# 32-column TensorE tiles from batch 1, sums in one bank, batch 2's sums via DRAM on two queues, and scores a quarter into a w_out group

## The chip, the cores and the metric

One core of a Trainium2 chip runs the whole program. The metric is device time in microseconds (us); "span" is the stretch from the first to the last instruction in the profile, which is about 2 us shorter than the time. One run of the kernel before differs from the next by some 0.3 us, so differences of 1 us count here.

## The reference, cut to what matters

```python
# 8 batches, 8 heads, 1024 tokens, head size 64; 64 projected keys
k_proj, v_proj = E @ k, F @ v                       # per head: 64 x 64
attn = softmax(q @ k_proj.T / 8)                    # 1024 x 64 per head
x = (attn @ v_proj), heads side by side             # 8192 tokens x 512
h = x @ w_in                                        # 512 -> 2048
out = (h * clip(h + 3, 0, 6) / 6) @ w_out           # 2048 -> 512
```

By far the most work is in the two products with w_in and w_out: 32 and 8 groups per batch, 256 rounds of a 128x128 by 128x512 product (a round is the time in which all tiles that lie side by side do one matmul each). The attention of the next batch is woven in between.

## The kernel before

The dense products go through one helper. It cuts the stationary operand into column tiles, which run side by side in the array (the tile form in the views, such as 128*64, is rows by columns):

```python
width = [P // 2]                                    # 64 columns
def in_columns(ps, stationary, moving, **flags):
    for lo in range(0, stationary.shape[-1], width[0]):
        nc.tensor.matmul(ps[lo:lo + width[0]], stationary[:, lo:lo + width[0]], moving, **flags)
```

The softmax denominators are made in two ways. In the "visits" (batches 1 and 2) they are summed with 64x64 matmuls against ones, straight into the layout that the products need. From batch 3 on each head's sum is made once, and the reciprocals go through DRAM and come back as broadcasts:

```python
def all_sums(self, alloc):                          # 8 matmuls of 32 columns, two banks
    ...
def spread(self, den):
    few = att.tile([P, 2, TOK], f32, ...)
    inverse(few, den)                               # Ln and Exp(-x) on ScalarE
    rows = dram.tile([H, NB, TOK], f32, ...)
    nc.sync.dma_start(out=rows..., in_=few[::16])
    self.recs = [rec_tile() for _ in range(KO)]
    for h in range(H):                              # 8 x 256 KB, all from the SP queue
        nc.sync.dma_start(out=self.recs[h // 2]..., in_=rows[h:h + 1]....to_broadcast([D, NB * TOK]))
```

Loads are chained: `turn` transposes a batch's keys (kT) and queries (qT) by DMA, waits for them on GpSimd ("mark"), and only then lets the loads of the next batch start. In block b TensorE does w_in and w_out of batch b, and the attention of batch b + 1 sits at fixed places n = 0 to 7 between the groups.

The softmax here doesn't subtract the row's maximum and nothing guards it: scores larger than these inputs give would overflow.

## Time and profile before

| | kernel before |
|---|---|
| time, median of 3 | 507.14 us (507.04 to 507.15) |
| span | 505.5 us |
| TensorE busy / VectorE / ScalarE | 99% / 48% / 51% |
| instructions of the program, in 16 KB fetches | 38 |

The busy share says that TensorE never rests, and not what it does: a change of tile form or a slower round counts as busy. The lines that show where TensorE loses time stand in the prediction.

```profile
q8 instruction: 38, 0.62, 0.5%
```

### The profile page before, as it was taken

The numbers are of one execution on the slowest core, as the hardware profiler recorded it, in microseconds if no ns is written. First come the engines' busy times: TensorE is split into PE (matmuls) and PEld (weight loads), VectorE is DVE, ScalarE is ACT, GpSimd is POOL, SyncE is SP. The second block draws the span as 40 slices with busy tenths as digits, with TensorE's granted clock in tenths as the row PEclk, the third lists the DMA queues.
The fourth block names the chain that finished last, engine by engine and source line by source line (L and its number), as shares of the span: only waits on it lengthen the run. The fifth ranks groups of instructions, "written<-read, shape, count | busy, mean of one in ns | idle before, by whom it ended". The sixth has DMA issues, their size and how long they took to land.

```text
span 505.5 us, 11242 instructions
## 1 busy us (share of the span) xinstructions
PE 498.9 (99%) x4858; PEld 259.5 (51%) x4858; DVE 245.1 (48%) x384; ACT 256.1 (51%) x438; POOL 38.7 (8%) x58
## 2 busy tenths in 40 slices
PE   8999999999999999999999999999999999999997
PEld 4554554554454555545554555545555555555554
DVE  3572736865733564536635455533752446334420
ACT  3757466566565444653555544654455544344431
POOL 8620020020020020020001000000000000000000
PEclk9999999999999999999999999999999999999999
DMA  9999979799299999699416992248110361101112
GB/s 168 198 205 208 200 131 231 142 155 202 73 151 194 230 169 190 137 154 249 123 43 118 205 249 69 61 100 209 43 43 29 82 164 43 39 26 43 43 43 84
DMA packets 78074, 66.30 MB, mean 131 GB/s; under 512 B 36216, under 2 KB 67192, under 8 KB 78024
## 3 DMA queue, kind: packets, MB, share of 16 engines
q0 software_dynamic: 32480, 29.36, 37.4%
q1 hardware_dynamic: 45320, 35.89, 27.7%
q8 instruction: 38, 0.62, 0.5%
q10 hardware_dynamic: 224, 0.33, 0.2%
q14 instruction: 12, 0.10, 0.1%
HBM read 69.73 MB, written 16.94 MB: 171 GB/s over the span
## 4 chain that ended last, share of the span: by engine, by line
PE 85%; DMA 12%; POOL 2%; ACT 1%; issue 0%; DVE 0%; ACTq 0%; POOLq 0%
PE mm L172 79%; DMA q<-in_q_dram 6%; DMA w_in_sb<-in_moe_w_in_dram 2%; PE at L172 2%; DMA v<-in_v_dram 2%; DMA qT<-q 2%; PE at L251 1%; PE at L233 1%; PE mm L251 1%; POOL q L106 1%; PE mm L271 1%; POOL k L110 1%; ACT aT L242 0%; PE mm L233 0%; POOL v L110 0%
## 5 line engine op out<-in xcount | busy, mean ns | idle before, releaser
L512 DVE SCALAR_TENSOR_TENSOR g<-r,mm 128x512 bf16<-128x512 f32 x256 | 173.5, 686 | 178.7 <-ACT r L511 177.9
L172 PE MATMUL mm<-w_out_sb,g 128*64 128x512 bf16 (+2 forms) x2080 | 235.0, 376 | 0.2 <-DVE g L512 0.2
L172 PE MATMUL mm<-xT,w_in_sb 128*64 128x512 bf16 x2048 | 231.5, 379 | 0.3
L511 ACT ACTIVATE r<-mm 128x512 f32<-128x512 f32 x256 | 152.2, 599 | 74.5 <-PE mm L172 73.5
L172 PEld LDWEIGHTS <-w_in_sb 128*64 128x64 bf16 x2048 | 117.2, 110 | 104.0 <-issue 0.8
L172 PEld LDWEIGHTS <-g 128*64 128x64 bf16 x2080 | 116.2, 110 | 105.5 <-issue 7.0
L546 ACT COPY o_sb<-mm 128x512 f32<-128x512 f32 x55 | 32.2, 586 | 126.7 <-PE mm L172 126.7
L264 DVE TENSOR_TENSOR xT<-at,rec 128x512 bf16<-128x512 f32 x42 | 26.5, 681 | 6.5 <-ACT rec L184 6.5
L242 ACT ACTIVATE aT<-at 128x512 bf16<-128x512 f32 x38 | 20.2, 615 | 9.1 <-PE at L233 9.1
L208 DVE CAST kp<-at 64x512 bf16<-64x512 f32 x12 | 7.7, 677 | 15.9 <-PE at L172 15.9
L223 POOL COPY mark<-qT 1x1 bf16<-1x1 bf16 x4 | 0.7, 176 | 165.0 <-DMA qT<-q 165.0
L242 ACT ACTIVATE aT<-mm 128x512 bf16<-128x512 f32 x18 | 10.3, 613 | 3.9 <-PE mm L233 3.9
L546 DVE COPY o_sb<-mm 128x512 f32<-128x512 f32 x8 | 5.5, 687 | 13.8 <-PE mm L172 13.8
L172 PE MATMUL at<-v,f_t 128*64 128x512 bf16 x48 | 11.4, 381 | 0.3 <-DMA v<-in_v_dram 0.3
L172 PE MATMUL at<-k,e_t 128*64 128x512 bf16 x48 | 11.6, 382 | 0.0
L264 DVE TENSOR_TENSOR xT<-mm,rec 128x512 bf16<-128x512 f32 x14 | 9.0, 685 | 4.3 <-PE mm L251 4.3
L184 ACT ACTIVATE rec<-rec 128x1024 f32<-128x1024 f32 x10 | 10.6, 1060 | 0.3
L178 ACT ACTIVATE rec<-mm 128x512 f32<-128x512 f32 x10 | 5.5, 595 | 7.9 <-PE mm L251 5.4
L178 ACT ACTIVATE few<-mm 128x512 f32<-128x512 f32 x10 | 5.4, 594 | 7.4 <-PE mm L271 7.4
L93 PE MATMUL mm<-ones 128*128 128x512 bf16 x18 | 7.4, 549 | 1.5 <-DVE halves L84 1.5
L172 PEld LDWEIGHTS <-e_t 128*64 128x64 bf16 x56 | 5.7, 110 | 6.0 <-issue 1.8
L211 DVE CAST vp<-at 64x512 bf16<-64x512 f32 x12 | 8.3, 694 | 0.4
(73 smaller groups left out, 155.0 us busy)
## 6 DMA issues: line engine op xcount, KB each, us to landing
out_dram<-o_sb SPq DMA_DIRECT2D x63, 256.0 KB, 3.0
rec<-rows SPq DMA_DIRECT2D x40, 256.0 KB, 6.5
k<-in_k_dram POOLq DMA_DIRECT2D x7, 1024.0 KB, 15.0
v<-in_v_dram POOLq DMA_DIRECT2D x7, 1024.0 KB, 20.7
q<-in_q_dram POOLq DMA_DIRECT2D x7, 1024.0 KB, 10.0
w_out_sb<-in_moe_w_out_dram POOLq DMA_DIRECT2D x4, 512.0 KB, 16.0
w_in_sb<-in_moe_w_in_dram POOLq DMA_DIRECT2D x5, 256.0 KB, 9.7
k<-in_k_dram POOLq DMA_DIRECT2D x4, 256.0 KB, 5.5
```

The lines of the kernel that those rows point to most:

```text
L93: nc.tensor.matmul(ps, ones[:, :P], ones, start=True, stop=True)
L172: nc.tensor.matmul(ps[lo:lo + width[0]], stationary[:, lo:lo + width[0]], moving, **flags)
L178: nc.scalar.activation(rec[:, i], den, AF.Ln)
L184: nc.scalar.activation(flat, flat, AF.Exp, scale=-1.0)
L208: nc.vector.tensor_copy(self.kp[:, :, a, :], self.ps[:KP].rearrange("p (h d) -> p h d", d=D))
L211: nc.vector.tensor_copy(self.vp[a * KP:(a + 1) * KP], self.ps[KP:].rearrange("p (h d) -> p h d", d=D))
L242: nc.scalar.activation(self.aT[j][:, r].rearrange("p a n -> p (a n)"), tiles[r], AF.Exp, scale=scale)
L251: nc.tensor.matmul(tiles[t][c:c + D].rearrange("p (r n) -> p r n", r=2), stationary(r, 2 * j + a), self.aT[j][r:r + KP, :, a, :], start=Tr ...
L264: nc.vector.tensor_mul(self.xT[:, j, t, :], av[t], rec[:, t])
L511: nc.scalar.activation(r, h_ps, AF.Relu, bias=0.5, scale=1.0 / 6.0)
L512: nc.vector.scalar_tensor_tensor(g[:, fo, :], r, 1.0, h_ps, op0=ALU.min, op1=ALU.mult)
L546: (copy or nc.scalar.copy)(o_sb, o_ps)
```

## The change

Its intent, as far as the code tells, is to give the sums the same tile form as the dense products, so that they need no change of form, to use the cheaper sums for batch 2 too, and to place the attention pieces where ScalarE has time to follow. Cut to its core, with long calls put in words:

```diff
-    halves = consts.tile([P, NB, KP // 4], ...)
+    halves = consts.tile([P, 2, 2, NB, KP // 8], ...)   # all heads' sums in one bank
...
+    width[0] = P // 4                # from batch 1: 32 columns
     second = Attention(2)
     for b in range(1, B):
...
-        if b == 1: visits(...) for batch 2
+        if b == 1:
+            plan = {4: (4, second.all_scores), 5: (3, second.all_sums), 6: (2, second.first_values),
+                    7: (2, lambda: second.some_values((2, 3), ((pmm, pmm), (pmm, pat))))}
+        elif b + 1 < B:
+            plan = {3 + (b == 2): (2, third.projected) ..., 4 + (b == 2): (2, values 0, 1), 6: (2, values 2, 3)}
+            if b == 2:
+                plan.update({0: (2, second.projected), 1: (4, second.all_scores), 2: (4, second.all_sums)})
+            else:
+                plan.update({0: (1, scores 1, 2, 3), 1: (4, second.all_sums)})
...
             for h in range(H):
-                nc.sync.dma_start(out=self.recs[...]
+                (nc.sync, nc.gpsimd)[h % 2].dma_start(out=self.recs[...]
...
-        if fo == 7:
+        if fo == 9:
             second.projected()       # batch 1, in block 0
```

In the plan, `n: (q, act)` means: act after quarter q of the n-th w_out group. The transpose of batch 3's queries moves from the middle of block 1 to its end, batch 1's first scores come one quarter later, and the loads of batches 5 to 7 bring keys and values before queries.

## The prediction

> **What bounds the kernel now.** I read the page's busy times and granted clock first, then the chain that ended last, then TensorE's rows in order of time, because only these show what lies between two matmuls.
>
> ```profile
> PE 498.9 (99%) x4858; PEld 259.5 (51%) x4858; DVE 245.1 (48%) x384; ACT 256.1 (51%) x438; POOL 38.7 (8%) x58
> PEclk9999999999999999999999999999999999999999
> PE 85%; DMA 12%; POOL 2%; ACT 1%; issue 0%; DVE 0%; ACTq 0%; POOLq 0%
> L172 PE MATMUL mm<-w_out_sb,g 128*64 128x512 bf16 (+2 forms) x2080 | 235.0, 376 | 0.2 <-DVE g L512 0.2
> L172 PE MATMUL mm<-xT,w_in_sb 128*64 128x512 bf16 x2048 | 231.5, 379 | 0.3
> ```
>
> TensorE is busy 99% at full clock, VectorE and ScalarE about half. The chain is TensorE too; its DMA share is the start, up to the queries of batch 1 at 68.7 us. A saving must therefore come out of TensorE's own row: its pace inside dense stretches, the loss where the kind of matmul changes, or the few waits. The timeline of TensorE (start, length, line, operation, tile form, count) has the first two:
>
> ```profile
> 299.78 3.62 PE L172 MATMUL mm<-xT,w_in_sb 128*64 128x512 bf16 x32
> 303.23 1.89 PE L172 MATMUL mm<-w_out_sb,g 128*64 128x512 bf16 x16
> 305.05 0.41 PE L251 MATMUL mm<-aT,vp 64*64 64x512 bf16 x4
> 305.29 0.39 PE L251 MATMUL at<-aT,vp 64*64 64x512 bf16 x4
> 305.51 0.39 PE L233 MATMUL at<-qT,kT 64*64 64x256 bf16 x8
> 305.83 1.92 PE L172 MATMUL mm<-w_out_sb,g 128*64 128x512 bf16 x16
> 307.58 0.60 PE L172 MATMUL mm<-xT,w_in_sb 128*64 128x512 bf16 x4
> ```
>
> Pace: 32 matmuls, in 16 rounds of two 64-column tiles side by side, go from 299.78 to 303.23: 0.2157 us a round. Change of form: 8 rounds from 303.23 should end at 304.955, but the values start at 305.05, 0.10 lost. Two rounds of values take 0.46 where 0.43 is due: 0.02 for the first round after a change. Two rounds of scores (256 columns, 0.109 each) and another 0.10 lead to 305.83; the 8 rounds after that take 1.75 instead of 1.725, again 0.02. An excursion out of the dense form and back costs 0.10 + 0.02 + 0.10 + 0.02, about 0.245 us.
>
> ```profile
> 152.66 1.89 PE L172 MATMUL mm<-w_out_sb,g 128*64 128x512 bf16 x16
> 154.49 0.61 PE L271 MATMUL mm<-aT,halves 128*32 128x512 bf16 x8
> 155.03 0.63 PE L251 MATMUL at<-aT,vp 64*64 64x512 bf16 x8
> 155.59 1.92 PE L172 MATMUL mm<-w_out_sb,g 128*64 128x512 bf16 x16
> ```
>
> Here the sums (32-column tiles) and the values make two forms in one excursion, with three changes. The sums take 0.54 to the next start: two rounds (0.43), one change (0.10) and 0.01 for the first round, not 0.02. Such an excursion costs about 0.357 us. Last, the waits:
>
> ```profile
> 54.70 0.38 PE L172 MATMUL at<-k,e_t 128*64 128x512 bf16 x1
> 55.42 0.38 PE L172 MATMUL at<-v,f_t 128*64 128x512 bf16 x1 [0.34 <-DMA v<-in_v_dram]
> 68.80 0.41 PE L233 MATMUL mm<-qT,kT 64*64 64x256 bf16 x8 [0.27 <-DMA qT<-q]
> 382.26 3.97 PE L172 MATMUL mm<-xT,w_in_sb 128*64 128x512 bf16 x32
> 386.39 3.64 PE L172 MATMUL mm<-w_out_sb,g 128*64 128x512 bf16 x32 [0.16 <-DVE g L512]
> ```
>
> 0.50 us for batch 1's values at 54.7, 0.34 for its queries at 68.8, and 0.65 in the last batch's score exponentials: 16 rounds from 382.26 take 4.13 instead of 3.47. A fourth of 0.17 lies inside the scores at 139.5.
>
> **What the Trainium skill says.** "TensorEngine Tiling (Array Packing)", Key Properties: changing the tiling mode, not just the tile, drains TensorE. The trace agrees: 0.10 us per change. "TensorE: Matmul & The Clock Gate", section "Wait — 56ns, not 53.3ns?": back to back, a warm matmul costs N / 2.4 GHz plus some 2.5 ns. For 512 columns that is 215.8 ns, the measured pace; two tiles at 512 columns and four at 256 (0.109) both show it, so I take it as a cost per round, whatever the number of tiles. The same section gives a rival: with hardware decode off, the sequencer spends about 62 ns per matmul; no row here rules on it. "Trainium Kernel Development and Optimization", Key Constraints: DMAs issued from several engines run on the same 16 DMA engines, and only issue time is saved. In this trace the eight broadcasts of reciprocals take the SP queue 4.9 us to issue (340.8 to 345.8).
>
> **The change part by part.**
>
> *32-column tiles.* From batch 1 on, a dense round becomes four matmuls and four weight loads instead of two and two. The pace should stay at 0.2158, so 1800 rounds gain nothing. What changes is the form: the sums now have the form of the dense matmuls and cost no change. I counted excursions in the two programs' order of instructions, after batch 1's four visits (the same in both). Before: 15 plain and 5 with sums, 15 x 0.245 + 5 x 0.357 = 5.46 us. After: 18 plain ones, and six sums inside the dense stretches. Returning to 32 columns costs 0.01 instead of 0.02, as the sums show, so 18 x 0.231 = 4.16, plus one change from 64 to 32 columns, 0.11. Saved: 1.20 us.
>
> *Batch 2's sums.* 32 matmuls of 64x64 for sums (with the values, 8 rounds) become 8 of 32 columns plus 4 rounds of values: 2 rounds fewer, 0.43 us. Putting all sums in one bank halves the ScalarE work on them (a 0.59 and a 1.06 us instruction fewer per batch), which is off the path. The round trip through DRAM must now fit in block 1. Sums end about 115 us, the exponential about 118, rows written and visible 2 us later (338.85 to 340.82), and eight broadcasts of 256 KB in 8 to 11 us more: 129 to 131 for the last. VectorE wants the first half at 128 and the rest at 131. It just fits, because loading batch 3 (3 MB, begun at 101) is over by about 120 now that the transpose of its queries no longer runs beside it.
>
> *What it makes VectorE do at the start of batch 2.* Eight products at a pitch of 0.6 us stand behind the last hardswish, from about 128.5, so the third and fourth head pairs are ready 0.15 and 0.35 us after TensorE wants them. Before, a projection of 1.73 us lay there and hid this. Given back: 0.5 us.
>
> *Scores a quarter into a w_out group.* Twelve rounds (2.6 us) now follow the scores before w_in needs a bank. Six exponentials pitched at 0.49 us start 0.4 us after the first scores and end about when the group does. The 0.65 us of the last batch goes. The 0.17 of batch 3's scores goes too, but both new all-at-once scores use all eight banks, and the last waits about 0.17 for the copy of the output just made: 2 x 0.17 against 0.17, plus 0.17.
>
> *Batch 1.* Projecting two w_in tiles later removes the 0.50 us wait for values. But it ends 0.9 us later, so the transpose of the keys, then that of the queries on the same queue, are issued about 0.6 us later than 60.27, and the scores start near 69.4 instead of 68.8, with one more quarter (0.86) done before them. Net gain 0.28 us.
>
> Sum: -1.20 - 0.43 - 0.65 + 0.17 - 0.28 + 0.50 = -1.89 us. 507.14 - 1.89 = 505.25; I predict 505.2.
>
> **The rivals.** First, the sequencer cannot feed eight instructions per 216 ns. Proven over long stretches is only four per 216 (54 ns each); bursts such as 24 score matmuls with their loads in 0.78 us (16 ns each) could come from a filled queue. At 62 ns per matmul a round would take 248 ns, some 15% on 1800 rounds: about 565 us. Against it: the sums with four tiles and the scores ran at the array's pace. Second, four tiles hide the 2.5 ns of a round: 1800 x 2.5 = 4.5 us, so about 501. Against it: four-tile scores still pay it (0.109 and not 0.107). Third, batch 2's reciprocals come late. In this trace the time from writing the rows to the first broadcast was 2.0 to 5.9 us, the longer ones beside loads; 4 us late gives 507 to 509. Fourth, all small waits vanish, with the batch 1 gain as large as the two waits (0.84) and none at batch 2: 504.2.
>
> **Range and chances.** The removed changes and rounds (1.6 us) are nearly certain if the pace holds; the waits are worth between -1.6 and +1. So 503.6 to 506.8 holds it 8 times in 10. Faster by over 2% needs 10 us, which no part has: 0.02. Slower by over 2% needs the first rival: 0.04. Within 2%: 0.94.
>
> **What would show each step.** The dense pace in batches 4 to 6 should be 0.2158 per round of four; a cycle of one batch, 60.00 us before, should be 59.85. No gap beside the sums. TensorE near 382 without a wait, near 131 a short one on VectorE's xT. The first scores near 69.4. I am wrong if the pace per round moves by even 1 ns (1.8 us), or if TensorE waits for a broadcast.

## The result, and the profile after

| | before | after |
|---|---|---|
| time, median of 6 | 507.01 us (506.89 to 507.15) | 507.89 us (507.76 to 509.31) |
| span of the profiled run | 505.5 us | 505.8 us |
| time less span, profiled run | 1.75 us | 2.1 us |

The ratio is 1.0024 (95% interval 1.0011 to 1.0037): slower by a quarter of a per cent, where 0.4% faster was forecast. A ratio here is the mean time of one kernel's runs over that of the other's of the same rounds, so it is not quite the ratio of the medians.

The page of the changed kernel: TensorE still is the chain, but broadcasts ("rec<-rows") have entered it, and the instruction queue has nearly doubled.

```profile
PE 496.9 (98%) x8562; PEld 246.2 (49%) x8562; DVE 245.7 (49%) x384; ACT 244.3 (48%) x425; POOL 51.4 (10%) x82
q8 instruction: 67, 1.10, 0.9%
PE mm L175 85%; PE at L175 2%; DMA rec<-rows 2%; DMA w_in_sb<-in_moe_w_in_dram 2%; DMA k<-in_k_dram 1%; DMA rows<-few 1%; PE mm L254 1%; PE at L236 1%; PE mm L236 1%; PE at L254 1%; PE mm L275 1%; PE at L422 0%; POOL rec L290 0%; POOL q L109 0%; POOL k L113 0%
```

First the part of the prediction that held. TensorE's timeline in block 4 of the changed kernel (start, length, line, operation, tile form, count):

```profile
263.06 3.63 PE L175 MATMUL mm<-xT,w_in_sb 128*32 128x512 bf16 x64
266.51 3.63 PE L175 MATMUL mm<-w_out_sb,g 128*32 128x512 bf16 x64
269.96 0.61 PE L275 MATMUL mm<-aT,halves 128*32 128x512 bf16 x8
270.40 1.90 PE L175 MATMUL mm<-xT,w_in_sb 128*32 128x512 bf16 x32
```

64 matmuls, 16 rounds of four, take 3.45 us: 0.2157 a round, as with two tiles. The sums take 0.44, two rounds and nothing for a change. The starts of the single matmuls in the trace give 0.21583 in both kernels. A cycle of one batch (scores at 259.68 to scores at 319.54) is 59.86 us; 60.00 before.

The last batch's scores, a quarter into the group, no longer stop TensorE (16 rounds from 382.78 take 3.46, where the kernel before needed 4.13):

```profile
380.18 2.77 PE L175 MATMUL mm<-w_out_sb,g 128*32 128x512 bf16 x48
382.78 3.63 PE L175 MATMUL mm<-xT,w_in_sb 128*32 128x512 bf16 x64
386.24 3.63 PE L175 MATMUL mm<-w_out_sb,g 128*32 128x512 bf16 x64
```

Now what did not. TensorE at the start of block 2, where batch 2's products are needed:

```profile
128.85 1.91 PE L175 MATMUL mm<-w_out_sb,g 128*32 128x512 bf16 x32
132.63 1.48 PE L175 MATMUL mm<-xT,w_in_sb 128*32 128x512 bf16 x24 [1.87 <-DVE xT L267]
134.67 1.69 PE L175 MATMUL mm<-xT,w_in_sb 128*32 128x512 bf16 x28 [0.56 <-DVE xT L267]
```

Eight rounds from 128.85 end at 130.58, but the next start is at 132.63: 2.04 us. The six rounds from there end at 133.94, and the next start is at 134.67: 0.73. Together 2.77 us. The bracket names VectorE's products, so look there, for what VectorE waited for:

```profile
127.78 1.28 DVE L267 TENSOR_TENSOR xT<-at,rec 128x512 bf16<-128x512 f32 x2
130.16 1.29 DVE L267 TENSOR_TENSOR xT<-at,rec 128x512 bf16<-128x512 f32 x2 [1.10 <-DMA rec<-rows]
131.88 1.29 DVE L267 TENSOR_TENSOR xT<-mm,rec 128x512 bf16<-128x512 f32 x2 [0.43 <-issue]
133.93 0.69 DVE L267 TENSOR_TENSOR xT<-mm,rec 128x512 bf16<-128x512 f32 x1 [0.75 <-DMA rec<-rows]
134.53 0.68 DVE L267 TENSOR_TENSOR xT<-at,rec 128x512 bf16<-128x512 f32 x1
```

VectorE waits for broadcasts in front of the third product and of the seventh. (The 0.43 in front of the fifth ended just after another broadcast had landed, at 131.80.) And the SP queue shows why these are late:

```profile
117.52 0.53 SPq L286 DMA_DIRECT2D rows<-few  x1
122.21 2.38 SPq L290 DMA_DIRECT2D rec<-rows  x4
```

The reciprocals are written at 117.52, but the first broadcast, which waits until they are in DRAM, is issued at 122.21: 4.7 us, where I had 2.0. In the trace's DMA packets the loads of batch 3 run from 102.3 to 122.3 us, and the broadcasts' packets from 123.8 to 132.3.

### The profile page after: what moved, and what is told of

The parts are those of the page before. It is cut to its first block, busy times and chain, and to the rows that moved or that the text cites. A ratio compares the mean times of both kernels' runs of the same rounds, so it can differ in the third digit from the quotient of the medians. Undisturbed runs are those within 1.5% of the kernel's fastest.

```text
span 505.8 us, 18693 instructions
## 1 busy us (share of the span) xinstructions
PE 496.9 (98%) x8562; PEld 246.2 (49%) x8562; DVE 245.7 (49%) x384; ACT 244.3 (48%) x425; POOL 51.4 (10%) x82
## 4 chain that ended last, share of the span: by engine, by line
PE 92%; DMA 6%; POOL 1%; issue 1%; ACT 0%; DVE 0%; POOLq 0%; DVEq 0%; ACTq 0%
PE mm L175 85%; PE at L175 2%; DMA rec<-rows 2%; DMA w_in_sb<-in_moe_w_in_dram 2%; DMA k<-in_k_dram 1%; DMA rows<-few 1%; PE mm L254 1%; PE at L236 1%; PE mm L236 1%; PE at L254 1%; PE mm L275 1%; PE at L422 0%; POOL rec L290 0%; POOL q L109 0%; POOL k L113 0%
## 5 line engine op out<-in xcount | busy, mean ns | idle before, releaser
L175 PE MATMUL mm<-w_out_sb,g 128*32 128x512 bf16 (+3 forms) x3904 | 235.9, 376 | 0.0
L175 PE MATMUL mm<-xT,w_in_sb 128*32 128x512 bf16 (+1 forms) x3840 | 231.5, 379 | 2.8 <-DVE xT L267 2.4
L175 PEld LDWEIGHTS <-w_in_sb 128*32 128x32 bf16 (+1 forms) x3840 | 110.2, 98 | 113.6 <-issue 4.1
L175 PEld LDWEIGHTS <-g 128*32 128x32 bf16 (+1 forms) x3904 | 109.4, 98 | 111.5 <-issue 6.7
L290 POOL DMA_DIRECT2D rec<-rows x24 | 12.5, 531 | 194.1 <-DVE g L511 159.3
L267 DVE TENSOR_TENSOR xT<-at,rec 128x512 bf16<-128x512 f32 x31 | 19.9, 683 | 6.9 <-ACT rec L187 5.8
L267 DVE TENSOR_TENSOR xT<-mm,rec 128x512 bf16<-128x512 f32 x25 | 16.2, 687 | 6.2 <-PE mm L254 4.9
L175 PE MATMUL at<-k,e_t 128*32 128x512 bf16 (+1 forms) x104 | 13.3, 379 | 0.0
L175 PE MATMUL at<-v,f_t 128*32 128x512 bf16 (+1 forms) x104 | 13.2, 379 | 0.0
L175 PEld LDWEIGHTS <-e_t 128*32 128x32 bf16 (+1 forms) x104 | 5.8, 98 | 5.9
```

Of the source, the lines that this page charges most:

```text
L267: when(lambda t=t: nc.vector.tensor_mul(self.xT[:, j, t, :], av[t], rec[:, t]))
L290: (nc.sync, nc.gpsimd)[h % 2].dma_start(out=self.recs[h // 2][h % 2 * D:(h % 2 + 1) * D].rearrange("d t n -> d (t n)"), in_=by_head[h // 4 ...
```

## The experiments

Three theories stood against each other at first. Theory: batch 2's reciprocals come late, because the loads of batch 3 hold the DMA engines. Rival A: VectorE's eight products in a row are the wait, whenever the reciprocals come. Rival B: 32-column tiles cost something.

**1. Batch 3's loads queued earlier** (the edit in short):

```diff
-                nc.gpsimd.tensor_copy(mark, last)
-                load_kqv(self.b + 1, "qkv" if self.b == 2 else "kvq")
+                if self.b != 2: (mark; load_kqv(self.b + 1, "kvq"))
+                if self.b == 1: load_kqv(3, "qkv")
```

> The changed kernel, but the loads of batch 3 are queued right behind those of batch 2 instead of after the transpose of batch 2's keys. Theory (batch 2's reciprocals come late because the loads of batch 3 hold the DMA engines until 122.3 us, so the rows written at 117.5 are only visible at 122.1): the loads end near 112, the rows are visible about 2 us after their issue, the broadcasts end 2 to 3 us earlier, TensorE's waits at 130.6 to 134.7 fall from 2.8 to about 0.5 us, and the time to 505.7. Rival A (VectorE's eight products in a row make TensorE wait, whenever the reciprocals come): waits and time unchanged, 507.9. Rival B (32-column tiles cost something that the trace hides): unchanged as well.

Measured: 516.97 us, ratio 1.0192. The total is a miss by 11 us, the mechanism is not. The loads ended at 112.2 us and held up the transposes of batch 2 instead: issuing that of the queries took 19.93 us (5.38 in the changed kernel), and that of the keys stands behind it:

```profile
114.94 0.64 PE L239 MATMUL mm<-qT,kT 64*64 64x256 bf16 x8 [8.09 <-DMA kT<-kp]
```

TensorE lost 8.3 us there, and some 3 us more because its granted clock was 0.50 from 110.6 to 120.8 (rounds 0.427 us apart). But once past it, with no loads left, the round trip is quick, on the SP queue:

```profile
128.34 0.53 SPq L289 DMA_DIRECT2D rows<-few  x1
130.15 2.38 SPq L293 DMA_DIRECT2D rec<-rows  x4
```

and the wait at block 2 is small:

```profile
139.66 1.91 PE L175 MATMUL mm<-w_out_sb,g 128*32 128x512 bf16 x32
141.72 1.48 PE L175 MATMUL mm<-xT,w_in_sb 128*32 128x512 bf16 x24
```

1.8 us instead of 4.7 from write to broadcast; 139.66 plus eight rounds is 141.39, so 0.33 us of waiting instead of 2.77. Rival A falls: VectorE has the same eight products here, and none waits for a broadcast. Those 0.3 us are what they cost by themselves; I had put them at 0.5.

**2. The projection of batch 3 at the end of block 1.** TensorE has 1.73 us of work that needs no reciprocals; the kernel before had it in this place.

```diff
-                plan.update({0: (2, second.projected), 1: ...
+                plan.update({1: ...
...
         if b == 1:
             later.append(lambda: qT_dma.update({3: q_transposed(3)}))
+            third.projected()
```

> The changed kernel, but the projection of batch 3 (1.73 us of TensorE that needs no reciprocals) stands at the end of block 1, where the kernel before had it, instead of inside the first w_out group of block 2. Theory and rival A: it fills 1.7 of the 2.8 us of waiting, 506.2 us. Rival B: the wait is not what costs, 507.9.

Measured: 505.88 us (505.70 to 507.91), ratio 0.998 (0.9966 to 0.9993). As expected, within 0.4 us; the waits left at block 2 add up to 0.4 us. Rival B can't explain that.

**3. Batch 3's values loaded twice.** Meant as the suspected cost, doubled; the result stays right.

```diff
                 load_kqv(self.b + 1, "qkv" if self.b == 2 else "kvq")
+                if self.b == 2:
+                    nc.gpsimd.dma_start(out=kqv[3]["v"], in_=kqv_dram["v"][3])
```

> The changed kernel with the values of batch 3 loaded twice: 1 MB more in front of the round trip, the suspected cost doubled. Theory: the extra load takes 5 to 6 us of the DMA engines at the rate seen there (about 330 KB in 2 us), so the last broadcast lands 4 to 6 us later and the time goes to 512 to 514. Rival A and B: unchanged within 0.5 us.

Measured: 517.56 us (516.56 to 518.95), ratio 1.0205: the right direction, but about twice the size. The edit did not do what I meant. The second load writes the tile that the first one fills, so GpSimd waited until the first had landed. It issued the second only when the rows had been written (4.69 us, as in the changed kernel), and in front of its own four broadcasts on the same queue:

```profile
123.47 0.88 POOL L229 DMA_DIRECT2D v<-in_v_dram  x1 [19.90 <-DMA v<-in_v_dram]
124.34 2.13 POOL L292 DMA_DIRECT2D rec<-rows  x4
```

The four broadcasts of the SP queue landed at 126.1 to 133.6 us, hardly later than in the changed kernel (125.8 to 132.5). The packets of GpSimd's four began only at 133.9, when most of the second load's (125.6 to 136.6) were done, and the last one ended at 140.8 us instead of 132.3. The wait had moved forward, into the values of block 1, because a PSUM bank (of the memory that TensorE writes) is not free until VectorE's first products have read it:

```profile
128.54 0.62 PE L256 MATMUL mm<-aT,vp 64*64 64x512 bf16 x6
139.22 0.63 PE L256 MATMUL at<-aT,vp 64*64 64x512 bf16 x2 [10.06 <-DVE xT L269]
```

VectorE's first product, which needs a broadcast from each queue, started at 138.5, not at 127.8. After so long a wait the granted clock was 0.50 until 144.7. So this run shows what late broadcasts cost TensorE; that a load delays the rows it does not test.

**4. 64 columns all through, the rest as changed.**

```diff
-    width[0] = P // 4
+    width[0] = P // 2
```

> The changed kernel with 64-column tiles all through. Theory (a round costs the same with either width; narrower tiles save changes of form only): 18 excursions at 0.245 and 6 for the sums at 0.23 instead of 18 at 0.231 and one change of width: 5.8 instead of 4.3 us, 1.5 more, of which some 0.3 is taken back from the wait at batch 2, which TensorE then reaches later: 509.1. Rival B (32 columns cost time): below 507.5.

Measured: 507.51 us (507.45 to 508.82), ratio 1.001. A miss by 1.6 us, and at first sight it speaks for rival B. The row of TensorE says otherwise. The sums now cost a change each way (0.54 us from their start to the next, with 64-column tiles on both sides, instead of 0.43), so between the projection of batch 4 and the last matmul this kernel is 1.0 us slower than the changed one (168.89 to 502.22 against 169.67 to 501.96). It wins elsewhere: the wait at block 2 is 1.13 us instead of 2.77, TensorE gets there 0.64 us later and the rows took 3.84 us instead of 4.69 to reach DRAM; and the stretch from the last matmul's start to the end of the span is 3.2 instead of 3.8 us. That last difference is no matter of tiles, as runs 8, 11 and 12 show.

**5. All broadcasts on one queue.**

```diff
-                (nc.sync, nc.gpsimd)[h % 2].dma_start(...
+                nc.sync.dma_start(...
```

> The changed kernel with all eight broadcasts of each batch issued from the SP queue. Theory: the broadcasts are bound by the DMA engines (8.5 us from the first packet to the last in the changed kernel, as in the kernel before on one queue, 9.2), not by their issue, so the wait at batch 2 stays within 1 us of 2.8. If the 0.35 us by which the changed kernel's time exceeds its span more than before's does (507.9 - 505.8 against 507.25 - 505.5) comes from the broadcasts on the GpSimd queue, it goes: 507.5 or a little less. Rival (two queues are what keeps the reciprocals nearly in time): the wait grows by 2 us or more, above 509.

Measured: 508.20 us (507.71 to 508.51), ratio 1.0015; before was at 507.21 in these rounds. The total is a miss by 0.7 us. The wait at block 2 was 2.2 us (TensorE came there 0.8 us later), and the broadcasts' packets took 9.2 us instead of 8.5: two queues buy little. The time exceeds the span by 1.8 us, as in the kernel before, and not by 2.1. That the median did not fall may have to do with the end: in this profile, the slowest of the four runs, the tail (from the start of the last matmul to the end of the span) takes 4.5 us.

**6. The kernel before with 32 columns and nothing else.**

```diff
+    width[0] = P // 4
     second = Attention(2)
```

> The kernel before with 32-column tiles from batch 1 on and nothing else. Theory: only changes of form are saved: 15 plain excursions at 0.236 (measured in the changed kernel) instead of 0.245, and 5 with sums at 0.236 instead of 0.357, less one change of width (0.11): 0.6 us, so the last matmul starts 0.6 us earlier and the time is 506.4 to 506.7. Rival B (32 columns cost time that the trace hides): 507.2 or more.

Measured: 509.44 us (508.69 to 510.10), ratio 1.0043. A clear miss: 2.2 us slower instead of 0.6 faster. TensorE's own row is as expected (each sum saves 0.12 us, the pace is 0.2158), but it waits for the values of batch 5:

```profile
202.54 0.39 PE L172 MATMUL at<-k,e_t 128*32 128x512 bf16 x2
204.80 0.39 PE L172 MATMUL at<-v,f_t 128*32 128x512 bf16 x2 [1.87 <-DMA v<-in_v_dram]
```

These are 2.0 us beyond a round. Before, the last packet of those loads started at 201.2 us and was needed at 202.3: the chain from reciprocals to transposes to loads had about 1 us to spare, which no share of busy time shows. Here it is 3.5 us late at the mark behind the transposes (182.1 against 178.7 us). The other addition is the tail, 4.0 instead of 3.2 us.

**7. Batch 2 in visits, as before; the rest as changed.**

```diff
-            plan = {4: (4, second.all_scores), 5: (3, second.all_sums), ...
+            plan = {4 + i: (2, lambda i=i: ends.append(second.visit(i, third))) for i in range(3)}
+            plan[7] = (4, lambda: second.visit(3, third)())
```

> The changed kernel with batch 2's sums, reciprocals and values done on the chip in four visits as in the kernel before, and batch 3's projection at the end of block 1; all else as changed. Theory (the wait for batch 2's reciprocals through DRAM is what eats the gain): the 2.8 us of waiting go, two rounds of sums (0.43) and one more excursion (0.24) come back, so 2.1 us less than the changed kernel: 505.8. Rival: 507.5 or more.

Measured: 508.02 us (506.80 to 510.64), ratio 1.0025. By the median a miss: 2.2 us above what was expected, and within what the rival allowed, but the six runs spread over 3.8 us. The profiled run, the fastest, shows no wait at block 2, but 0.9 us before the scores of batch 3 at 147.7 us, for the transposed queries, and a tail of 4.4 us. So the wait at block 2 did go, and other losses came in its place; where the slower runs lost up to 3.8 us more isn't known, since they have no profile.

**8. Run 2 and, in addition, 96 TensorE instructions fewer.** In the trace's DMA packets the last 16 KB of instructions arrive from 502.33 to 503.32 us in the changed kernel, while the last output goes out (packets from 502.81). In the kernel before the last fetch was over at 501.33, 1.8 us ahead of the output's packets. Leaving a few early tiles at 64 columns shortens the program, so that this fetch is no longer due.

```diff
-    width[0] = P // 4
...
             for fo in range(FO):
+                if (b, t, fo) == (1, 0, 6):
+                    width[0] = P // 4
```

> The run with batch 3's projection moved to the end of block 1 (505.9 us), and now the first six w_in tiles of block 1 keep 64 columns: 96 TensorE instructions fewer, so that the last fetch of a 16 KB block of instructions, which falls on the last output's transfer (500.2 to 501.5 beside 500.6 to 502.4), is no longer due before the program ends. Theory: from the issue of the last large output to its semaphore takes 1.9 us as before and not 3.1, so 0.8 to 1.2 us less: 504.7 to 505.1. Rival (the longer tail has to do with the narrower tiles or the second queue): unchanged, 505.9.

Measured: 505.98 us (505.28 to 508.29), ratio 0.9983 (0.9967 to 0.9999). In the time a miss: no better than run 2 within the scatter. In the trace a hit: 66 fetches instead of 67, the last output takes 1.88 us from issue to semaphore (3.07 in run 2, 1.84 before), the tail 3.19 us (4.28 in run 2). This profiled run had begun 0.37 us later at batch 1's scores, which hides a part.

**9 and 10. The kernel before with 32 columns in blocks 1 to 3 only, and from block 4 on only.** Run 6 left open whether narrow tiles delay the loads.

```diff
     for b in range(1, B):
+        width[0] = P // 4 if b < 4 else P // 2      # run 9; run 10: if b >= 4
```

> The kernel before with 32-column tiles in blocks 1 to 3 only (the widths are 64 again from block 4). In the run with 32 columns everywhere TensorE waited 2.0 us for batch 5's values at 202.5 us, and the kernel before had not waited there. Theory C (twice the TensorE instructions mean twice the 16 KB instruction fetches, which hold up the DMAs of the chain reciprocals - transposes - loads): the wait at 202.5 stays, 1.3 us or more, and the time is 508.3 or more. Rival D (that chain had hardly any slack, and it was late by chance or by some other part): no wait, about 0.2 us saved, 506.9 to 507.2. In both the tail after the last matmul is 3.2 us as before, because the last group has 64 columns.

> The kernel before with 32-column tiles from block 4 on only. Theory (a dense round costs the same; only changes of form are saved): three sums inside the dense form (0.12 each) and some 9 plain excursions (0.009 each), less the one change of width (0.11): 0.3 us faster, 506.8 to 507.0, no wait at 202.5, and a tail of 3.2 us because no fetch of instructions falls on the last output with this count of instructions. Rival B (32 columns cost time): 507.5 or more.

Measured: run 9 at 509.20 us (506.89 to 511.38), ratio 1.0037; the profile has the wait at 202.2 us again (2.0 us) and a tail of 3.2. Five of the six runs were at 508.5 or more, one at 506.9. Run 10 at 507.08 us (507.00 to 507.76), ratio 1.0000, four of the five runs within 507.0 to 507.2 and no such wait in the profile. Its profiled run is the slowest of the five: it waited 1.7 us for batch 1's queries at 69.5, before any tile is narrow, so they are not the cause. So narrow tiles in blocks 1 to 3 go with the late loads, and in blocks 4 to 7 they cost nothing that shows, though the 0.3 us that they should save doesn't show either.

Rival D (chance alone) is unlikely: 9 of 10 runs with narrow tiles there are late, and of all runs of the kernel before, 29, one is above 507.9 (508.23, in the rounds of runs 9 to 12). Theory C (the fetches) fits the packets: in both late profiles a fetch of 1 us falls on the write of the rows (159.5 and 160.0 us; rows to first broadcast 4.6 and 4.7 us, before 3.4), and another, at 165.4, on the one broadcast whose issue took 1.05 and 1.55 us instead of 0.6. In the kernel before and in run 10 there was no fetch between 158 and 171 us. This is a coincidence in time, seen in two profiles, and was not tested apart. For it speaks that in the changed kernel a fetch alone did delay the rows (the count stands below); against it, that one trip of run 10 with a fetch in it took 1.97 us all the same.

**11. Run 8 with all broadcasts on the SP queue.**

> The best version so far (projection of batch 3 at the end of block 1, the last instruction fetch moved off the last output) with all broadcasts on the SP queue. Theory: the 0.3 us outside the span go (they went in the run with one queue: 508.5 - 506.7), the rest stays: 505.4 to 505.8, against 506.0. Rival (two queues bring the reciprocals earlier): 506.5 or more.

Measured: 505.35 us (504.50 to 505.96), ratio 0.9961 (0.9949 to 0.9973). As expected, and faster than both kernels. Time less span is 1.8 us, the tail is 3.2 us and nothing at block 2 or elsewhere in the dense part waits over 0.13 us.

**12. The changed kernel with only the shorter instruction stream** (the edit of run 8 alone).

> The changed kernel with 64 columns in the first six w_in tiles of block 1, nothing else: 96 TensorE instructions fewer, so that the last instruction fetch does not fall on the last output. Theory: the tail after the last matmul takes 3.2 us and not 3.8, and the time is 507.1 to 507.3; the wait at batch 2 stays at 2 to 3 us. Rival: 507.9.

Measured: 507.53 us (506.82 to 510.44), ratio 1.0023. The tail is 3.18 us as expected, the wait at block 2 is still there (1.45 in front of the values, 0.79 after). The median gains 0.36 of the 0.6 expected; two of six runs are near 510, unprofiled.

## Why the prediction was wrong, point by point

The step that failed is the round trip of batch 2 through DRAM: "rows written and visible 2 us later", "It just fits, because loading batch 3 ... is over by about 120". The exponential was done in time, at 117.5. But I took the 2.0 us from a place where no load was in flight (338.85 to 340.82), and the end of the loads from a rate that the trace did not keep: they went on until 122.3 (123.3 in the kernel before, so taking the transpose away gained 1 us). The rows took 4.7 us, the last broadcast landed at 133.85, and the eighth product could start only at 134.5. TensorE waited 2.77 us for these products, where 0.5 had been allowed.

It was the third rival, with its own figure from the trace (2.0 to 5.9 us), that came true. That its 507 to 509 holds the result is partly luck: 0.9 us of the result are the tail and the time outside the span, which this rival did not have.

Runs 1 and 2 show the step: without loads beside it the trip takes 1.8 us and the wait falls to 0.33, and with other work in its place most of the loss goes. Run 3 shows that still later broadcasts cost still more.

One thing is mixed in. In the changed kernel a fetch of instructions ran from 120.98 to 122.03 us, beside the write of the rows, and in run 1 neither a load nor a fetch was there. The kept traces tell the two apart. In the changed kernel and its variants 41 trips, from the rows to the first broadcast, fell where no load was in flight: the 24 without a fetch took 1.81 to 1.95 us, the 17 with one took 2.15 to 3.84. So a fetch alone delays the rows too. Run 4, with half the instructions, had no fetch after 117.81 but loads until 121.0, and batch 2's rows took 3.84 us: loads without a fetch account for about 1.9 of the 2.7 us that this trip was too long. Whether the fetch took all of the rest isn't shown: in run 11 the rows took 4.64 us with loads until 122.5, and its fetch was over at 120.67.

The sum of the prediction, term by term, from the two profiled runs:

| term | predicted | measured |
|---|---|---|
| changes of form and first rounds after them | -1.20 | -1.04 (5.38 to 4.34 from 82.7 us on) |
| two rounds fewer for batch 2 | -0.43 | -0.43 (count of instructions, pace unchanged) |
| last batch's exponentials | -0.65 | -0.65 |
| all-at-once scores | +0.17 | -0.02 (two waits of 0.08, one of 0.17 gone) |
| batch 1's values and queries | -0.28 | -1.05 |
| start of batch 2 | +0.50 | +2.91 (2.77, and 0.14 for a bank at 128.5) |
| tail after the last matmul | not seen | +0.59 (3.22 to 3.81) |
| outside the span | not seen | +0.35 (1.75 to 2.1) |

These add up to +0.66; the profiled times differ by 507.90 - 507.25 = +0.65. The exactness is luck: the changed kernel also started 0.12 us earlier, and nobody knows such sums to 0.1.

- *32-column tiles: right in the pace, right in the change of form.* The first rival (the sequencer can't feed eight instructions per round) and the second (2.5 ns hidden) both fell: 0.21583 us a round. The way out of the 32-column form costs 0.102 to 0.104 us instead of 0.097, so an excursion is 0.236, not 0.231. But I had no eye for what twice the instructions mean elsewhere: 67 fetches instead of 38, one of them on the last output and one beside the rows of batch 2.
- *Batch 1: the mechanism was right, the size off.* The transpose was issued 0.65 us later, as predicted (60.92), but took 7.3 us until the mark and not 8.4, so the scores started at 68.49 without a wait. From the profile after:

```profile
66.66 1.89 PE L175 MATMUL mm<-w_out_sb,g 128*64 128x512 bf16 x16
68.49 0.41 PE L236 MATMUL mm<-qT,kT 64*64 64x256 bf16 x8
```

  That is 0.31 earlier with 0.86 more work done, less the 0.12 of an earlier start. The fourth rival had counted 0.84 of this, the two waits. The other 0.2 is a misread line of the prediction: the first matmul of the keys, at 54.70, ran alone, so that the wait for the values cost a round on top of its 0.50 us.
- *Scores a quarter into the group: right.*
- *The tail was missed altogether.* Runs 8, 11 and 12 give 3.2 us with 66 fetches; all runs with 67 fetches have 3.8 to 4.5.
- *So was the cost outside the span.* Runs 5 and 11 have all broadcasts on SP and 1.7 to 1.8 us; the changed kernel and runs 1 to 4, 8 and 12, with half of them on the GpSimd queue, have 2.1 to 2.3. But run 7, which has batch 2 in visits and uses the GpSimd queue from batch 3 on, has only 1.8 to 1.9, so that queue by itself isn't the cause. What is done in those 0.3 us is not in the profile.
- *The range.* It was drawn as if the change were one on TensorE's row alone. It should have been as wide as the DMA chain is uncertain: single runs of the changed kernel spread over 1.5 us, and of some experiments over 3 to 4.5.

What stays open: how much of the rows' 4.7 us was the fetch, why narrow tiles in blocks 1 to 3 make the loads late in most runs (fetches, argued from two profiles), what the 0.3 us outside the span are, and where the slow runs of runs 7, 9 and 12 lost their time.

## What to carry to other kernels

When one engine is at 99%, price a change first on that engine's own row, round by round, but then list every transfer that must land within a microsecond or two of its use, and ask what else will be in the DMA engines at that moment. A round trip through DRAM is to be priced under load, and placed where work that doesn't need it (here a projection) lies in front of its use. Count the instructions too: twice as many are twice as many fetches, and one that fell on the last output here lengthened the tail by 0.6 to 1.3 us.

## What the Trainium skill lacked or had wrong

- "Advanced Engine Details and Errata", ISA Cache, has the 16 KB line of 256 instructions, and the trace agrees (67 packets of 16,384 B for 17,124 TensorE instructions, 8562 matmuls and as many weight loads). It lacks that a fetch, about 1 us long here, can hold up a data transfer that falls on it: the last output took 1.8 to 1.9 us from issue to semaphore without and 2.5 to 3.3 with a fetch beside it, and the rows' trip, with no load in flight, 1.8 to 1.95 without and 2.15 to 3.8 with one.
- "TensorE: Matmul & The Clock Gate", Part 3, "The mechanism", says in its list that weight loads overlap matmuls in flight only where the row group differs. As it stands this does not hold here: all four column tiles use all 128 rows, each weight load takes 98 ns, and rounds still follow at 0.21583 us, so the loads are hidden. (The text above that list names the background weight buffer as a second way; whether it is the one at work, no run shows.) The page also lacks the sustained pace of four column tiles, and that it equals that of two.
- "TensorEngine Tiling (Array Packing)", Key Properties, has the drain at a change of mode without its size: 0.097 to 0.104 us here, plus 0.024 us for the first round of 64-column tiles and 0.010 for 32.
- "Trainium Kernel Development and Optimization", Key Constraints, says that several issuing engines only save issue time. The runs agree in the main (packets 8.5 us on two queues, 9.2 on one), but no page has the 0.3 us of time outside the span that is there in every run with batch 2's broadcasts on the GpSimd queue and in no other.
- No page gives the time from a small write to DRAM until it may be read while large loads are under way: 3.4 to 6.0 us here, against 1.8 to 2.0 with neither load nor fetch beside it.
